# Sums of w_in earlier on VectorE, one first-layer block behind the x transposes of units 2 and 3, and values and masks of units 4 to 7 in another order

## The chip, the core and the metric

One core of one Trainium2 chip runs the whole program. The core has a matrix engine (TensorE; its matmuls are called PE in the profile, its weight loads PEld), VectorE (DVE), ScalarE (ACT), GpSimd (POOL) and SyncE (SP), each with its own instruction queue, and 16 DMA engines that carry the transfers which POOL, SP and ACT issue. The metric is the device time of one execution in microseconds. A change under about 0.3% can't be told from none here.

## What is computed

The inputs q, k and v have the shape (8, 8, 576, 64): batch, heads, positions, head dimension. Attention looks at a window of 32 positions on both sides. Its output, one row of 512 per token, goes through a two-layer network with a GELU in its sigmoid form.

```python
scores = scale * np.matmul(q, k.transpose(0, 1, 3, 2))
mask = np.abs(pos[:, None] - pos[None, :]) <= 32
attn = softmax(np.where(mask, scores, -1e9))
x = np.matmul(attn, v).transpose(0, 2, 1, 3).reshape(4608, 512)
h = x @ w_in                              # 512 x 2048
g = h * (1.0 / (1.0 + np.exp(-1.702 * h)))
out = g @ w_out                           # 2048 x 512
```

## The kernel before

**Units and tiles.** The 4608 tokens are cut into 36 units of 128 and 9 tiles of 512 (four units). For a unit `u` the steps are: `scores(u)` (24 small matmuls, then two exponentials on ACT, one for each half of the heads, which write the tile `p`), `band(u)` (VectorE multiplies `p` by the 0/1 mask), `values(u)` (TensorE multiplies `p` with the values), `norm(u)` (VectorE divides by the row sums and writes `x`), and a transpose of `x` into `xT`. Each unit is worked in blocks of 64 positions, so `values(u)` needs the values twice: `ve[u % 9]`, the 128 rows as loaded, and `vo[u % 5]`, the 128 rows from 64 further on. `odd_v(u)` makes `vo` with two copies: rows 64 to 127 of `ve[u]`, and rows 0 to 63 of `ve[u + 1]`.

**PSUM.** Every accumulator lies in one of seven named places: `t` (two banks) and `A`, `C`, `B`, `E`, `LA`, `LB`. A step that writes one must wait until the last reader of the step before it in that place is done. `scores(u, "t")` and `values(u, "t")` take `t`; with `"AC"` they take A and C, one for each half of the heads.

**The first layer.** Tile 0 goes through `layer1_plain(0, d, half, tag)` (line 378): eight matmuls for 256 of the 2048 hidden columns (block d of 0 to 7) and 256 of the tile's tokens, then a GELU on ACT. In `opening`, `l1(half, *ds)` calls it with the places of the list `h` in turn. From tile 1 on, `l1_group` (line 407) computes with seven products instead of eight. Four of these need sums of w_in, the tiles `a1` to `a4`, and sums of x (`xs`). `w1_sums((i,), half)` (line 327) makes half of one of the four with one VectorE instruction. Half 0 reads the chunks 0 and 2 of w_in (512 columns each), half 1 the chunks 1 and 3. The first use of the sums is in the first group of tile 1.

**The second layer.** For tile 0 `self.l2` is a list of 64 steps of one matmul each, worked off by `self.do(self.l2, n)` between other work. The steps 0 to 7 need chunk 0 of w_out (`w2`), 8 to 15 chunk 1, 16 to 23 chunk 2, 24 to 31 chunk 3.

**What sets the order.** The program is written in a manual schedule: each engine executes its instructions in the order in which the code calls them, and waits in that order. So the position of a call in `opening` (line 562) is its position on every engine that it uses, and an instruction that waits holds back everything behind it on its engine.

**Loads.** q, k, v, w_in and w_out are loaded and converted by DMAs that POOL issues in program order. In the program's list of waits eight completion counters take turns, so every such load waits, before it is issued, for the load that stands eight places before it on POOL. The loads around the change are, in this order: w_in chunk 3, v 5, v 6, w_out chunk 0, v 7, v 8, w_out chunks 1, 2, 3, k 8, q 8 (two pieces), k 9, v 9, q 9, k 10, v 10.

**The stage of the change.** `opening` builds tile 0 (units 0 to 3) and the attention of tile 1 (units 4 to 7). Its second half, from line 644 on, runs: block 4 of half 0, the transposes of x of units 2 and 3 (`x_T2`, line 313, copied to `xT` by VectorE), the two copies `k_first` and `v_first`, then the blocks of half 1 between the transposes of tile 1's k and q (`T_four`, line 181: 32 transposes, two copies each), block 5 of half 0, scores of units 4 and 5, the blocks 6 and 7, the scores of units 6 and 7, eight steps of layer 2, then the masks, values and norms of units 4 to 7, two more blocks, and the transposes of x of units 4 to 7. Then `first_layer1` (line 847) begins tile 1's first layer.

Of the kernel before, what the change touches and what calls it, by code (L numbers as in the profile page):

```python
# [26 lines left out]
class _Kernel:  # L27
# [166 lines left out]
    def load_v(self, u):  # L194
        if u >= self.NU:
            return
        t = self.ve[u % 9]
        for off, b, s, n in self.pieces(128 * u, 128):
            self.nc.gpsimd.dma_start(t[off:off + n, :, :self.D], self.v[b, :, s:s + n, :].rearrange("h s d -> s h d"))  # L199

    def odd_v(self, u, eng):

        vo = self.vo[u % 5]
        nxt = self.v_first if u == self.NU - 1 else self.ve[(u + 1) % 9][0:64]

        def words(ap):
            return ap.rearrange("p h d -> p (h d)").bitcast(I32)

        eng.tensor_copy(words(vo[64:128]), words(self.ve[u % 9][64:128]))  # L209
        eng.tensor_copy(words(vo[0:64]), words(nxt))  # L210
# [351 lines left out]
    def opening(self):  # L562

        nc, dve, act, pool = self.nc, self.nc.vector, self.nc.scalar, self.nc.gpsimd
        self.setup()
        dve.memset(self.idle, 0.0)
        dve.memset(self.spark, 0.0)
        for t in self.ve:
            dve.memset(t[:, :, self.D:], 1.0)
        self.load_first("k", 0)  # L570
        self.load_first("q", 0)
        make_identity(nc, self.ident)
        act.activation(self.spark, self.spark, AF.Exp)
        for u in (0, 1, 2):
            self.load_v(u)
        self.load_w1(0)
        self.setup_mask()
        self.load_first("k", 1)
        self.load_first("q", 1)
        self.cut_mask()  # L580
        self.load_w1(1)
        self.load_v(3)
        self.load_v(4)
        self.load_w1(2)
        self.load_four("k")
        self.load_four("q")
        self.load_w1(3)
        self.odd_v(3, pool)
        dve.tensor_copy(self.identh, self.ident)
        self.keep_busy(60, "E", 96)  # L590
        self.T_first("k", 0, "AC", (dve, act))
        self.keep_busy(6, "E")
        self.T_first("q", 0, ("LA", "LB"), (dve, act))
        self.keep_busy(4, "E")
        for u in (5, 6):
            self.load_v(u)
        self.load_w2(0)
        for u in (7, 8):
            self.load_v(u)
        for c in (1, 2, 3):  # L600
            self.load_w2(c)
        self.load_kq("k", 8)
        self.scores(0, "t")
        self.scores(1, "AC")
        self.odd_v(0, dve)
        self.odd_v(1, dve)
        self.keep_busy(10, "E")
        self.band(0)
        self.band(1)
        self.values(0, "t")  # L610
        self.values(1, "AC")
        self.norm(0)
        self.norm(1)
        self.keep_busy(6, "E")
        self.x_T(0, "LA", act)
        self.keep_busy(4, "E")
        self.x_T(1, "LB", act)
        self.T_first("k", 1, "AC", (dve, dve))
        h, n, gelus = [], [0], []

        def l1(half, *ds):
            for d in ds:
                self.layer1_plain(0, d, half, h[n[0] % len(h)])
                n[0] += 1

        self.layer1_plain(0, 0, 0, "B", gelus)
        self.T_first("q", 1, ("LA", "LB"), (dve, act))
        self.layer1_plain(0, 1, 0, "E", gelus)
        h[:] = ["B", "E", "LB"]
        self.scores(2, "t")  # L630
        self.scores(3, "AC")
        self.layer1_plain(0, 2, 0, "LA", gelus)
        self.layer1_plain(0, 3, 0, "LB", gelus)
        self.do(gelus)
        self.band(2)
        self.odd_v(2, dve)
        self.band(3)
        self.keep_busy(4, "t")
        self.values(2, "t")
        self.norm(2)  # L640
        self.keep_busy(4, "A")
        self.values(3, "AC")
        self.norm(3)
        l1(0, 4)
        self.x_T2(2, "A", dve)
        dve.tensor_copy(self.k_first, self.kT[0][:, :, 0:64])
        dve.tensor_copy(self.v_first, self.ve[0][0:64])
        for u in (8, 9, 10, 11):
            self.fetch(u)
        l1(1, 0, 1)  # L650
        halo = self.kT[4]
        self.T_four("k", "AC", (dve, dve))
        dve.tensor_copy(self.kT[4][:, :, 0:64], halo)
        l1(1, 2, 3)
        l1(0, 5)
        self.T_four("q", "AC", (dve, act))
        l1(1, 4, 5)
        self.odd_v(4, dve)
        self.scores(4, "t")
        self.scores(5, "AC")  # L660
        for i in (3, 1, 2, 4):
            self.w1_sums((i,), 0)
        self.odd_v(5, dve)
        for d, tag in ((6, "B"), (7, "E")):
            self.layer1_plain(0, d, 0, tag, gelus)
        self.do(self.l2, 3)
        self.scores(6, "t")
        self.do(self.l2, 3)
        self.scores(7, "AC")
        self.do(gelus)  # L670
        self.do(self.l2, 2)
        self.band(4)
        self.band(5)
        self.odd_v(6, dve)
        self.odd_v(7, dve)
        self.band(6)
        self.values(4, "t")
        self.norm(4)
        self.band(7)
        self.values(5, "AC")  # L680
        self.norm(5)
        self.do(self.l2, 8)
        self.values(6, "t")
        self.norm(6)
        self.values(7, "AC")
        self.norm(7)
        h[:] = "BE"
        n[0] = 0
        for i in (3, 1):
            self.w1_sums((i,), 1)  # L690
        l1(1, 6, 7)
        self.x_T2(4, "A", act)
        self.do(self.l2, 4)
        self.x_T2(6, "t", dve)
        self.do(self.l2, 4)
# [218 lines left out]
```

## Time and profile before

| what | us |
|---|---|
| median of three runs (lowest, highest) | 287.91 (287.08, 288.02) |
| the profiled execution | 287.27 |
| its span in the trace | 285.5 |
| PE busy in the span | 275.4 |
| DVE busy | 217.1 |
| ACT busy | 193.7 |
| POOL busy | 128.3 |

The granted TensorE clock was 0.997 of full speed. The profile has these views: busy time and the chain of work that ended last; a timeline (start, duration in us, engine, line, operation, output<-inputs, and in brackets the idle time of that engine before it with what ended the wait); busy times of all engines in chosen windows; and the DMA issues. A row that ends in xN merges N like instructions. A row of POOL with DMA_DIRECT2D is the issuing of a load, and not its transfer: the landing shows only in what waits for it.

### The profile page before, as it was taken

The page shows a single profiled execution, that of the slowest core. Times are in us where ns is not written, and L with a number is a line of the kernel's source. Part 1 is how long each engine was busy: PE and PEld are TensorE (multiplying, and loading weights), DVE is VectorE, ACT ScalarE, POOL GpSimd, SP SyncE. Part 2 cuts the span into 40 slices and gives each one's busy share as a digit, 9 for nine tenths or more (in the row PEclk, how much of TensorE's full clock was granted, in tenths as well). Part 3 has the DMA queues.
Part 4 walks back from the last instruction along what each step waited for, and adds up shares of the span by engine and source line. Part 5 has one row for each costly group of instructions (what it writes and reads, how often), then busy time and mean ns, then how long its engine had stood idle before and what let it go on. Part 6 is the DMA issues. An engine that isn't in the chain of part 4 may idle for free.

```text
span 285.5 us, 9217 instructions
## 1 busy us (share of the span) xinstructions
PE 275.4 (96%) x3818; PEld 230.0 (81%) x3818; DVE 217.1 (76%) x500; ACT 193.7 (68%) x340; POOL 128.3 (45%) x194
## 2 busy tenths in 40 slices
PE   7898999999999999999999999999999999999994
PEld 6676847776778888888888888888887888888883
DVE  1755898897887978797879787888778878945731
ACT  2565784789787769667966896588658865568410
POOL 8966546898588538948175819330110000000000
PEclk9999999999999999999999999999999999999998
DMA  8999999999999999999999999994422030101033
GB/s 94 185 193 199 183 205 156 191 123 129 121 147 151 163 149 193 162 186 134 194 133 208 125 195 99 200 110 115 130 57 82 16 110 21 73 2 73 2 112 115
DMA packets 146987, 37.38 MB, mean 131 GB/s; under 512 B 133888, under 2 KB 142592, under 8 KB 146944
## 3 DMA queue, kind: packets, MB, share of 16 engines
q0 software_dynamic: 104464, 18.42, 95.7%
q1 hardware_dynamic: 42032, 17.84, 34.0%
q8 instruction: 30, 0.49, 0.7%
q10 hardware_dynamic: 448, 0.52, 0.6%
q14 instruction: 13, 0.11, 0.1%
HBM read 36.83 MB, written 9.44 MB: 162 GB/s over the span
## 4 chain that ended last, share of the span: by engine, by line
PE 83%; DVE 6%; ACT 4%; POOL 2%; DMA 2%; issue 2%; POOLq 0%
PE h L70 38%; PE o L70 37%; PE pv L70 3%; PE sc L70 3%; DMA kq<-in_k_dram 2%; ACT p L256 2%; DVE x L294 1%; DVE p L264 1%; PE tp L322 1%; POOL ve L199 1%; PE tp L232 1%; DVE a L335 1%; DVE vo L209 1%; ACT g L419 1%; PE tp L189 1%
## 5 line engine op out<-in xcount | busy, mean ns | idle before, releaser
L419 ACT ACTIVATE g<-h 128x512 f16<-128x512 f32 x128 | 72.2, 598 | 36.2 <-PE h L70 35.4
L70 PEld LDWEIGHTS <-g 128*128 128x128 f16 x576 | 54.5, 98 | 9.7
L70 PEld LDWEIGHTS <-a 128*128 128x128 f16 x512 | 49.3, 97 | 11.3 <-issue 1.2
L70 PE MATMUL h<-xs,a 128*128 128x256 f16 x384 | 57.6, 272 | 0.4 <-DVE h L432 0.2
L70 PEld LDWEIGHTS <-w 128*128 128x128 f16 x512 | 48.9, 98 | 7.9 <-DVE xT L67 1.0
L70 PE MATMUL o<-w,g 128*128 128x256 f16 (+1 forms) x320 | 55.1, 294 | 0.0
L70 PE MATMUL h<-xT,w 128*128 128x256 f16 x384 | 54.0, 273 | 1.1 <-DVE xT L67 0.8
L199 POOL DMA_DIRECT2D ve<-in_v_dram x40 | 34.0, 853 | 34.5 <-issue 26.4
L70 PEld LDWEIGHTS <-gs 128*128 128x128 f16 x384 | 36.8, 98 | 5.2 <-issue 0.6
L256 ACT ACTIVATE p<-sc 128x512 bf16<-128x512 f32 x72 | 36.6, 621 | 3.2 <-PE sc L70 3.2
L70 PE MATMUL o<-b,gs 128*128 128x256 f16 x256 | 37.6, 273 | 0.5 <-ACT o L67 0.5
L70 PE MATMUL o<-b,g 128*128 128x256 f16 x256 | 37.3, 273 | 0.0
L432 DVE TENSOR_TENSOR h<-h,s 128x512 f32<-128x512 f32 x32 | 22.3, 698 | 18.6 <-PE h L70 18.4
L131 POOL DMA_DIRECT2D qst<-in_q_dram x35 | 28.1, 805 | 6.1 <-DMA w<-in_moe_w_out_dram 3.0
L131 POOL DMA_DIRECT2D kst<-in_k_dram x31 | 26.4, 855 | 7.9 <-DMA ve<-in_v_dram 3.6
L67 ACT COPY h<-h 128x512 f32<-128x512 f32 x32 | 18.9, 589 | 15.9 <-PE h L70 15.5
L294 DVE TENSOR_TENSOR x<-pv,rec 128x256 f16<-128x256 f32 (+1 forms) x53 | 27.5, 520 | 1.8
L264 DVE TENSOR_TENSOR p<-p,mask 128x1024 bf16<-128x1024 bf16 x36 | 24.6, 685 | 3.1 <-ACT p L256 3.1
L438 DVE TENSOR_TENSOR h<-h,s 128x512 f32<-128x512 f32 x32 | 22.4, 699 | 4.8 <-PE h L70 4.2
L209 POOL COPY vo<-ve 64x264 int32<-64x264 int32 x29 | 13.8, 478 | 26.3 <-PE pv L70 24.8
L67 ACT COPY s<-h 128x512 f32<-128x512 f32 x32 | 19.2, 599 | 1.4
L70 PE MATMUL h<-xs,w 128*128 128x256 f16 x128 | 19.2, 273 | 0.0
(85 smaller groups left out, 366.5 us busy)
## 6 DMA issues: line engine op xcount, KB each, us to landing
out_dram<-o_sb SPq DMA_DIRECT2D x33, 256.0 KB, 3.9
ve<-in_v_dram POOLq DMA_DIRECT2D x32, 128.0 KB, 7.1
kst<-in_k_dram POOLq DMA_DIRECT2D x25, 128.0 KB, 6.8
qst<-in_q_dram POOLq DMA_DIRECT2D x21, 128.0 KB, 6.6
w<-in_moe_w_in_dram POOLq DMA_DIRECT2D x4, 512.0 KB, 8.6
w<-in_moe_w_out_dram POOLq DMA_DIRECT2D x4, 512.0 KB, 12.9
qst<-in_q_dram POOLq DMA_DIRECT2D x7, 96.0 KB, 7.7
kq<-in_q_dram POOLq DMA_DIRECT2D x2, 256.0 KB, 6.0
```

The source lines that it names most:

```text
L67: (eng.copy if eng is self.nc.scalar else eng.tensor_copy)(out, in_)
L70: self.nc.tensor.matmul(out, lhsT, rhs, start=start, stop=stop, skip_group_check=True)
L131: self.nc.gpsimd.dma_start(t[off:off + n], src[b, :, s:s + n, :].rearrange("h s d -> s h d"))
L189: self.nc.tensor.transpose(tp[64 * (h % 2):64 * (h % 2) + 64, h // 2, j, :], src[:, 4 * i + h, j, :], self.ident)
L199: self.nc.gpsimd.dma_start(t[off:off + n, :, :self.D], self.v[b, :, s:s + n, :].rearrange("h s d -> s h d"))
L209: eng.tensor_copy(words(vo[64:128]), words(self.ve[u % 9][64:128]))
L256: self.nc.scalar.activation(p[:, eo].rearrange("k h s -> k (h s)"), sc[eo], AF.Exp, scale=self.scale)
L264: (eng or self.nc.vector).tensor_mul(pv, pv, msk.to_broadcast([128, 8, 2, SQ]))
L294: dve.tensor_mul(x[:, 4 * at:4 * (at + n), :].rearrange("p (b h) d -> p b h d", b=n), acc[:, :, :, :D], r.to_broadcast([128, n, 4, D]))
L419: act.activation(g[:, f, 256 * half:256 * half + 256], bank.rearrange("p (i n) -> p i n", i=2), AF.Gelu_apprx_sigmoid)
L432: dve.tensor_add(e, b, s7)
L438: dve.tensor_add(c, b, s7)
```

## The change

Five things move, in `opening`, and one helper is new; nothing is computed differently.

1. `l1(0, 5)`, block 5 of half 0 of tile 0, moves from behind `l1(1, 2, 3)` to directly behind `x_T2(2, "A", dve)`. The list of places grows from three (B, E, LB) to four (B, E, LB, LA).
2. The half-0 sums of w_in move: 3, 1, 2 to behind the copies `k_first` and `v_first`, 4 to behind the copies of tile 1's k. They stood between `odd_v(4)` and `odd_v(5)`.
3. The half-1 sums 3 and 1 move from behind `norm(7)` to behind `odd_v(5)`, which so moves forward itself.
4. `odd_v(6)` and `odd_v(7)` move ahead of `band(5)`; each later mask moves behind the norm of an earlier unit; the eight layer-2 steps between `values(5)` and `values(6)` become four there and four behind `norm(6)`.
5. The load of v 8 is cut into two of 64 rows, and chunk 1 of w_out is issued between the two.

```diff
+    def load_v_part(self, lo, n):
+        u, at = divmod(lo, 128)
+        t = self.ve[u % 9]
+        for off, b, s, m in self.pieces(lo, n):
+            self.nc.gpsimd.dma_start(t[at + off:at + off + m, :, :self.D],
+                                     self.v[b, :, s:s + m, :].rearrange("h s d -> s h d"))
...
         self.load_w2(0)
-        for u in (7, 8):
-            self.load_v(u)
-        for c in (1, 2, 3):
+        self.load_v(7)
+        self.load_v_part(1024, 64)
+        self.load_w2(1)
+        self.load_v_part(1088, 64)
+        for c in (2, 3):
             self.load_w2(c)
...
-        h[:] = ["B", "E", "LB"]
+        h[:] = ["B", "E", "LB", "LA", "B", "E", "LB", "LA"]
...
         l1(0, 4)
         self.x_T2(2, "A", dve)
+        l1(0, 5)
         dve.tensor_copy(self.k_first, self.kT[0][:, :, 0:64])
         dve.tensor_copy(self.v_first, self.ve[0][0:64])
+        for i in (3, 1, 2):
+            self.w1_sums((i,), 0)
...
         dve.tensor_copy(self.kT[4][:, :, 0:64], halo)
+        self.w1_sums((4,), 0)
         l1(1, 2, 3)
-        l1(0, 5)
         self.T_four("q", "AC", (dve, act))
         l1(1, 4, 5)
         self.odd_v(4, dve)
         self.scores(4, "t")
         self.scores(5, "AC")
-        for i in (3, 1, 2, 4):
-            self.w1_sums((i,), 0)
         self.odd_v(5, dve)
+        for i in (3, 1):
+            self.w1_sums((i,), 1)
...
         self.band(4)
-        self.band(5)
         self.odd_v(6, dve)
         self.odd_v(7, dve)
-        self.band(6)
+        self.band(5)
         self.values(4, "t")
         self.norm(4)
-        self.band(7)
+        self.band(6)
         self.values(5, "AC")
         self.norm(5)
-        self.do(self.l2, 8)
+        self.band(7)
+        self.do(self.l2, 4)
         self.values(6, "t")
         self.norm(6)
+        self.do(self.l2, 4)
         self.values(7, "AC")
         self.norm(7)
         h[:] = "BE"
         n[0] = 0
-        for i in (3, 1):
-            self.w1_sums((i,), 1)
         l1(1, 6, 7)
```

## The prediction, made before the result was known

> **What bounds the kernel now.** I read the page first (span, and the chain that ended last), then busy times in windows, to see in which stage TensorE is not full.
>
> ```profile
> span 285.5 us, 9217 instructions
> ...
> PE 83%; DVE 6%; ACT 4%; POOL 2%; DMA 2%; issue 2%; POOLq 0%
> ```
> ```profile
> 22.00:45.00 23.00, 21.21 (x360) 15.87 (x360) 18.16 (x41) 15.73 (x26) 11.26 (x15) 1.00 1.56 192
> 45.00:69.20 24.20, 24.18 (x206) 17.58 (x203) 20.61 (x39) 18.74 (x34) 22.34 (x30) 1.00 2.01 150
> ...
> 90.00:285.50 195.50, 191.31 (x2425) 165.50 (x2423) 150.87 (x350) 131.21 (x234) 61.97 (x94) 1.00 1.12 117
> ```
>
> The columns are the window, its length, then busy time of PE, PEld, DVE, ACT, POOL, clock, DMA. From 45 us on TensorE is the bound (24.18 of 24.20 us, then 191.31 of 195.50). Between 22 and 45 us, the stage of the change, it is idle for 1.79 us, and some of its busy time there is spread-out small matmuls that wait. Whatever reaches the end of this stage earlier passes on to the end, as long as the loads allow it. So the question is how much earlier the blocks 6 and 7 of half 1 start, which close the attention of units 4 to 7. The chain that ended last tells where that stands:
>
> ```profile
> 31.33 0.48 DVE kq L67
> ...
> 43.00 0.32 PE pv L70 x8
> 43.32 1.85 PE h L70 x16
> ...
> 45.62 0.86 PE o L70 x4
> ```
>
> Those two blocks are the 16 matmuls at 43.3; the chain comes to them over VectorE, from 31.33 on. Four layer-2 steps take 0.86 us. The first place where time is lost is seen on TensorE:
>
> ```profile
> 22.73 1.05 PE L70 MATMUL h<-xT,w 128*128 128x256 f16 x8 [0.27 <-ACT g L390]
> 23.61 0.61 PE L322 MATMUL tp<-identh,x 128*128 128x128 f16 x8
> 25.01 1.92 PE L70 MATMUL h<-xT,w 128*128 128x256 f16 x16 [0.79 <-DVE xT L67]
> 26.86 1.11 PE L189 MATMUL tp<-ident,o_sb 128*64 128x128 bf16 x32
> 27.90 2.79 PE L70 MATMUL h<-xT,w 128*128 128x256 f16 x24
> 30.62 1.11 PE L189 MATMUL tp<-ident,o_sb 128*64 128x128 bf16 x32
> 31.67 1.92 PE L70 MATMUL h<-xT,w 128*128 128x256 f16 x16
> 33.52 0.70 PE L70 MATMUL sc<-kq 64*64 64x64 bf16 x48
> ```
>
> After the x transposes (23.61) TensorE stands idle 0.79 us for VectorE's copy of xT. Block 5 is the third part of the 24 matmuls at 27.90.
>
> **Part 1: block 5 into the gap.** Eight such matmuls take 22.73 to 23.61, 0.88 us. In the new order they begin when the transposes end (25.01 less 0.79, 24.2) and end near 25.0, where the copy of xT lets the next block start anyway. Its weights are there (block 4, same chunk, runs at 22.73). The 24 matmuls become 16, so everything from 30.62 on may come 0.88 us earlier: q transposes at 29.74, scores of units 4 and 5 at 32.64. The longer list of places costs nothing: all four have been read by GELUs of earlier blocks, and layer 2, which takes LA and LB, comes after them.
>
> **Part 2: does VectorE keep up until the scores?**
>
> ```profile
> 25.00 0.28 DVE L647 COPY v_first<-ve 64x528 bf16<-64x528 bf16 x1
> 27.56 2.35 DVE L67 COPY kq<-tp 128x1024 bf16<-128x1024 bf16 x2 [2.28 <-PE tp L189]
> 29.84 0.21 DVE L653 COPY kq<-kq 128x256 bf16<-128x256 bf16 x1
> 31.33 1.22 DVE L67 COPY kq<-tp 128x1024 bf16<-128x1024 bf16 x1 [1.28 <-PE tp L189]
> 32.59 0.69 DVE L209 COPY vo<-ve 64x264 int32<-64x264 int32 x1
> 33.31 0.29 DVE L210 COPY vo<-ve 64x264 int32<-64x264 int32 x1
> 33.52 1.28 DVE L335 TENSOR_TENSOR a<-w 128x1024 f16<-128x1024 f16 x2
> ...
> 35.56 0.69 DVE L336 TENSOR_TENSOR a<-w,a 128x1024 f16<-128x1024 f16 x1
> 36.27 0.72 DVE L209 COPY vo<-ve 64x264 int32<-64x264 int32 x1
> ```
>
> Three sums take 33.52 to 35.56, 2.04 us. Behind v_first they fill 25.3 to 27.3 of an idle stretch that ends at 27.56: nothing is late; if they were slowed by half, the k copies would be 0.8 us late, and the cover behind them (below) would be used up. The fourth sum runs 30.05 to 30.75. The q copy, ready at 31.33 less 0.88, 30.45, so starts 0.3 us late and ends at 31.97; the scores want it at 32.64, so 0.6 us of cover is left. Then come `odd_v(4)`, `odd_v(5)` and two sums of half 1 (1.28): 0.98 + 1.0 + 1.28 = 3.3 us, until 35.3. The first mask can't start before that anyway:
>
> ```profile
> 35.53 4.03 ACT L256 ACTIVATE p<-sc 128x512 bf16<-128x512 f32 x8
> ```
>
> Eight exponentials, 0.504 us each, stand behind a table load and the GELUs of the blocks before; all of these come 0.88 us earlier, so they start at 34.65 and finish units 4, 5, 6, 7 at 35.66, 36.67, 37.67, 38.68. Units 6 and 7 reuse t, A and C, and `values(4)` waits for t, too: this chain on ACT gains 0.88 us and no more, however early VectorE is.
>
> **Part 3: masks, values, norms.**
>
> ```profile
> 38.55 0.30 DVE L209 COPY vo<-ve 64x264 int32<-64x264 int32 x1
> ...
> 39.73 0.68 DVE L264 TENSOR_TENSOR p<-p,mask 128x1024 bf16<-128x1024 bf16 x1
> 40.34 0.19 DVE L293 RECIPROCAL rec<-pv 128x8 f32<-128x8 f32 x1
> 40.56 0.69 DVE L294 TENSOR_TENSOR x<-pv,rec 128x512 f16<-128x512 f32 x1
> 41.17 0.68 DVE L264 TENSOR_TENSOR p<-p,mask 128x1024 bf16<-128x1024 bf16 x1
> 41.77 0.17 DVE L293 RECIPROCAL rec<-pv 128x4 f32<-128x4 f32 x1
> ...
> 42.86 0.20 DVE L293 RECIPROCAL rec<-pv 128x8 f32<-128x8 f32 x1
> ```
>
> From start to start: a mask 0.61 (39.73 to 40.34), a norm from t 0.83 (40.34 to 41.17), a norm from A and C 1.09 (41.77 to 42.86), four copies of `odd_v` 1.18 (38.55 to 39.73). In the new order: band 4 35.7 to 36.3; four copies to 37.5; band 5 to 38.1. `values(4)` starts when t is free (37.67, and about 0.15 on) and takes 0.6, so norm 4 starts at 38.45. From there VectorE has no gap: 0.83 + 0.61 (band 6) + 1.09 (norm 5) + 0.61 (band 7) = 3.14, to 41.6. `values(7)` needs that mask, takes 0.45 with the latency, and blocks 6 and 7 start at 42.15 in place of 43.25 (the row of the chain says 43.32, after the last values): **1.1 us earlier**. The half-1 sums are gone from behind norm 7; the two blocks on TensorE (1.85 us) covered their 1.28 us there, so that gives nothing more.
>
> **Part 4: loads and contention.**
>
> ```profile
> 19.93 0.41 POOL L209 COPY vo<-ve 64x264 int32<-64x264 int32 x1 [0.44 <-DMA ve<-in_v_dram]
> 20.40 0.40 POOL L210 COPY vo<-ve 64x264 int32<-64x264 int32 x1
> ...
> 35.15 0.58 POOL L131 DMA_DIRECT2D qst<-in_q_dram  x1 [1.18 <-DMA w<-in_moe_w_out_dram]
> 36.01 0.89 POOL L131 DMA_DIRECT2D kst<-in_k_dram  x1 [0.28 <-DMA ve<-in_v_dram]
> 37.10 0.88 POOL L199 DMA_DIRECT2D ve<-in_v_dram  x1 [0.21 <-DVE vo L209]
> 39.81 0.87 POOL L131 DMA_DIRECT2D qst<-in_q_dram  x1 [1.83 <-DMA w<-in_moe_w_out_dram]
> ```
>
> Since each issue waits for the load eight places before, these rows give landings: w_out chunk 0 at 35.1, v 7 at 36.0, v 8 by 37.1, chunk 1 at 39.8. `odd_v(6)` and `odd_v(7)` now want v 7 at 36.6 and the first half of v 8 at 37.2: both are there. The first layer-2 steps come at 35.0, with chunk 0 landing at 35.1, in front of scores that wait until 35.66 anyway: hidden. Steps 8 to 11 come at 39.0 and want chunk 1. It is passed by half a v load. A half load's price: v 3 ended POOL's wait at 19.93, and the first half of v 4 was there by 20.40, so at most 0.47 us; a whole one is about 0.9 (v 7). Chunk 1 so lands near 39.35, and steps 8 to 11 run to 40.25. `values(6)` follows, four more steps end at 41.5, still before band 7 (41.6): no cost. [...] POOL issues one load more (0.6 to 0.9 us), in time in which it waits; k 8 to k 9 are first used in the second group of the stage that begins at 45 us, and v 8's second half only for unit 8.
>
> VectorE's copies are another matter: 0.30 us with POOL at rest (38.55), but 0.72 beside POOL's issue of 36.01, and 0.69 at 32.59. In the new order POOL issues the two loads of 36 to 37.5 just beside the four copies that are now ahead of band 5. Bounds: no copy hit, 0; two hit, 2 x 0.42 = 0.84. Norm 4 waits for `values(4)` for 0.3 us after band 5, so 0 to 0.5 us of it reaches the path. I take 0.1 (one copy hit).
>
> **Sum.** 1.1 less 0.1: a gain of 1.0 us. On the profiled execution that is 287.27 - 1.0 = 286.3; its span would be 284.5. The median of the three runs lies 0.64 above it, the mean of all four executions is 287.57, and I set the gain against that mean: **286.6 us**.
>
> **Rivals.**
>
> *A: the contention takes more.* Two copies hit, 0.5 us on the path, and the fourth sum or the q copy a little late (cover 0.6): a gain of 0.5 to 0.8, 286.8 to 287.1. For: four copies beside two issues. Against: the copy at 33.31 ran in 0.29 although POOL was issuing.
>
> *B: slower, the values load becomes the wait.* `odd_v(7)` now stands ahead of band 5, and every later mask and norm stands behind it on VectorE. From 37.5 on each us by which the first half of v 8 lands late moves the whole chain by one. Break-even is a landing at 38.6; if the half load is only done with chunk 1 behind it (39.8), the chain is 2.3 us late less the gain of 1.1: 288.8. For: a load completes only with its last piece. Against: 37.1 for the whole of v 8 now.
>
> *C: a half load costs a whole.* Chunk 1 at 39.8: steps 8 to 11 end at 40.7, `values(6)` at 41.15, the other four steps at 42.05, then `values(7)`: 0.35 to 0.45 us of the gain goes, which leaves 0.6 to 0.7, 286.9. Against: the row of 20.40.
>
> *D: VectorE was the whole bound, as the chain paints it.* Then 2.6 us of sums off it give 2 us, 285.5. Against: the exponentials beside it.
>
> **How the numbers follow.** Forecast 0.55 (gain 0.85 to 1.2), A 0.22, C 0.08, B 0.09, D 0.06. 0.3% is 0.86 us: faster by more is the forecast and D, 0.61; within, A and C, 0.30; slower, B, 0.09. The range reaches down to 285.8 (a gain of 1.1 on the fastest run is 286.0, and a little of D) and up to 287.6 (A's 0.5 on the median is 287.4); B and most of D are left out.
>
> **What would show it.** In the new profile: no idle time of 0.79 on TensorE before the block at 25.0; the k copies still near 27.6; scores of unit 4 near 32.6; exponentials from 34.7; band 5 done by 38.6, and blocks 6 and 7 at 42.1 to 42.3. Copies of `vo` at 0.7 before band 5 speak for A; VectorE idle behind a DMA in `odd_v(7)` for B; TensorE idle at 39 to 39.9 on w_out for C. A gain at 45 us that is gone at 70 us would mean that the later loads, and not TensorE, set the pace.

## The result, and the profile after

The changed kernel takes 286.25 us in the median of seven runs (285.84 to 286.63); the kernel before 287.40 (286.83 to 288.02), also in the median of seven, three of which are those of the table above. The ratio is 0.9953 with a 95% interval of 0.9937 to 0.9969: 1.15 us less, beyond the 0.3% that can be told from no change. The profiled execution took 286.05 us with a span of 284.3, against 287.27 and 285.5.

TensorE's timeline of the changed kernel, in the stage that the prediction works on (start, duration, engine, line, operation):

```profile
22.84 1.05 PE L70 MATMUL h<-xT,w 128*128 128x256 f16 x8
23.73 0.61 PE L329 MATMUL tp<-identh,x 128*128 128x128 f16 x8
24.18 2.87 PE L70 MATMUL h<-xT,w 128*128 128x256 f16 x24
...
32.76 0.70 PE L70 MATMUL sc<-kq 64*64 64x64 bf16 x48
...
39.40 1.04 PE L70 MATMUL o<-w,g 128*128 128x512 f16 x4
...
42.53 0.72 PE L70 MATMUL h<-xT,w 128*128 128x256 f16 x5
```

The wait of 0.79 us is gone: 24 matmuls follow the transposes at 24.18. Since the whole stage starts 0.11 us later than in before, I measure from the first of these rows (block 4 of half 0) to the last (blocks 6 and 7 of half 1): 42.53 - 22.84 = **19.69 us**, in before 43.25 - 22.73 = **20.52**. So the stage gives 0.83 us in this pair of profiled runs. VectorE's timeline of the changed kernel tells where it could have been more:

```profile
25.32 1.28 DVE L342 TENSOR_TENSOR a<-w 128x1024 f16<-128x1024 f16 x2
26.64 0.69 DVE L342 TENSOR_TENSOR a<-a,w 128x1024 f16<-128x1024 f16 x1
27.68 2.36 DVE L67 COPY kq<-tp 128x1024 bf16<-128x1024 bf16 x2 [0.35 <-PE tp L189]
...
33.26 1.28 DVE L342 TENSOR_TENSOR a<-w 128x1024 f16<-128x1024 f16 x2
35.97 0.69 DVE L271 TENSOR_TENSOR p<-p,mask 128x1024 bf16<-128x1024 bf16 x1 [1.43 <-ACT p L263]
36.69 0.46 DVE L216 COPY vo<-ve 64x264 int32<-64x264 int32 x1
37.18 0.29 DVE L217 COPY vo<-ve 64x264 int32<-64x264 int32 x1
37.50 0.55 DVE L216 COPY vo<-ve 64x264 int32<-64x264 int32 x1
38.07 0.29 DVE L217 COPY vo<-ve 64x264 int32<-64x264 int32 x1
38.29 0.68 DVE L271 TENSOR_TENSOR p<-p,mask 128x1024 bf16<-128x1024 bf16 x1
38.89 0.19 DVE L300 RECIPROCAL rec<-pv 128x8 f32<-128x8 f32 x1
```

VectorE waits 1.43 us for the exponentials ahead of band 4 and has no gap from there to norm 4 (nor behind it, to the last mask); the four copies between band 4 and band 5 take 1.60 us (36.69 to 38.29). The chain that ended last runs through exactly these rows.

Of the 1.19 us by which the span is shorter, 0.72 are there where the next stage scores unit 8 (first two fences: before, then after) and 0.83 at 188 us; the rest comes between 188 and 216 us, which the prediction doesn't speak of:

```profile
69.24 0.70 PE L70 MATMUL sc<-qT,kT 64*64 64x64 bf16 x48
...
188.33 0.70 PE L70 MATMUL sc<-qT,kT 64*64 64x64 bf16 x48
...
214.49 0.60 PE L70 MATMUL h<-xs,a 128*128 128x256 f16 x4 [0.23 <-DVE h L432]
...
216.41 0.70 PE L70 MATMUL sc<-qT,kT 64*64 64x64 bf16 x48
```
```profile
68.52 0.67 PE L70 MATMUL sc<-qT,kT 64*64 64x64 bf16 x46
...
187.50 0.70 PE L70 MATMUL sc<-qT,kT 64*64 64x64 bf16 x48
...
213.30 0.60 PE L70 MATMUL h<-xs,a 128*128 128x256 f16 x4
...
215.22 0.70 PE L70 MATMUL sc<-qT,kT 64*64 64x64 bf16 x48
```

From the scores at 188 to those at 216 us before takes 28.08 us, after 27.72. No call of that part of the program is changed. TensorE waits in before for an addition of VectorE (`h<-h,s`, line 432). That addition follows ACT's copy of the product that it adds. ACT's and VectorE's rows for it, before and after:

```profile
212.67 0.58 ACT L67 COPY s<-h 128x512 f32<-128x512 f32 x1
```
```profile
213.74 0.70 DVE L432 TENSOR_TENSOR h<-h,s 128x512 f32<-128x512 f32 x1 [1.09 <-PE h L70]
```
```profile
211.83 0.59 ACT L67 COPY s<-h 128x512 f32<-128x512 f32 x1
```
```profile
212.55 0.70 DVE L439 TENSOR_TENSOR h<-h,s 128x512 f32<-128x512 f32 x1 [0.74 <-PE h L70]
```

In before the addition starts 1.07 us after that copy, in after 0.72: it is 0.35 us late in before, and nothing that it reads explains it.

### The profile page after: what moved, and what is told of

The parts are those of the page before. It is cut to its first block, busy times and chain, and to the rows that moved or that the text cites. A ratio compares the mean times of both kernels' runs of the same rounds, so it can differ in the third digit from the quotient of the medians.

```text
span 284.3 us, 9219 instructions
## 1 busy us (share of the span) xinstructions
PE 275.4 (97%) x3818; PEld 229.8 (81%) x3818; DVE 217.0 (76%) x500; ACT 193.7 (68%) x340; POOL 128.8 (45%) x195
## 4 chain that ended last, share of the span: by engine, by line
PE 87%; DVE 4%; ACT 3%; DMA 2%; issue 1%; POOL 1%; DVEq 0%; ACTq 0%; POOLq 0%
PE h L70 39%; PE o L70 37%; PE pv L70 4%; PE sc L70 3%; DMA ve<-in_v_dram 2%; DVE p L271 2%; DVE x L301 1%; ACT p L263 1%; PE tp L329 1%; ACT L263 1%; PE junk L70 1%; PE tp L189 1%; PE tp L239 1%; POOL ve L199 1%; ACT g L426 1%
## 5 line engine op out<-in xcount | busy, mean ns | idle before, releaser
L199 POOL DMA_DIRECT2D ve<-in_v_dram x39 | 33.3, 857 | 37.8 <-issue 30.8
```

## The experiments

Two theories stood behind them. The first is the prediction's, cut to size: block 5 in the gap is the stage's gain, and the copies ahead of band 5 lie on the path. The second came from the rows above: the 0.36 us that before loses late have to do with the two halves of v 8, the one part of the change that adds instructions. Rivals are named with each run. Executions of one kernel differ by 1 us and more (before beside c1_after: 286.89 to 289.04); in some profiled runs part of this is seen as TensorE's wait for late transposes by DMA after 100 us (0.37 us in c0_before, 0.43 in e3_oldmasks, 0.76 in e9_oddpool_one). So beside each time stand two lengths from the trace that this doesn't touch: the stage, and the stretch from 188 to 216 us. "Gap" is the time from VectorE's wait to the start of the addition near 214 us, by the trace's records of VectorE. The experiments were taken in three groups, each with runs of before beside it, and the group e4 to e7 on another chip than the other two: a time is to be compared within its group, or through the ratio. (The ratio on record is not exactly the quotient of the two medians.)

| run | stage, us | 188 to 216, us | gap, ns | median, us (runs) | before beside it | ratio (95%) |
|---|---|---|---|---|---|---|
| before, profiled | 20.52 | 28.08 | 415 | 287.40 (7) | | |
| after, profiled | 19.69 | 27.72 | 64 | 286.25 (7) | 287.40 | 0.9953 (0.9937 to 0.9969) |
| c0_before | 20.35 | 28.07 | 416 | 287.8 (1) | 287.39 | |
| e1_block | 19.76 | 28.07 | 416 | 286.88 (12) | 287.39 | 0.9985 (0.997 to 1.000) |
| e2_sums | 20.35 | 28.08 | 417 | 287.31 (12) | 287.39 | 0.9998 (0.9981 to 1.0016) |
| e3_oldmasks | 19.48 | 27.71 | 65 | 286.42 (7) | 287.39 | 0.9959 (0.9941 to 0.9977) |
| e4_wholev8 | 19.54 | 28.07 | 417 | 286.83 (10) | 288.00 | 0.9955 (0.9933 to 0.9977) |
| e5_vo6early | 19.24 | 27.72 | 65 | 286.65 (12) | 288.00 | 0.9954 (0.9928 to 0.9981) |
| e6_oddpool | 18.72 | 27.72 | 65 | 285.74 (7) | 288.00 | 0.9914 (0.9886 to 0.9943) |
| e7_block_split | 19.73 | 27.71 | 65 | 285.97 (6) | 288.00 | 0.9921 (0.9895 to 0.9947) |
| e8_one_more | 20.35 | 27.72 | 64 | 287.11 (12) | 287.44 | 0.9991 (0.9972 to 1.0009) |
| e9_oddpool_one | 18.73 | 27.72 | 65 | 285.53 (11) | 287.44 | 0.9943 (0.9925 to 0.9960) |
| c1_after | 19.75 | 27.72 | 65 | 286.10 (6) | 287.44 | 0.9952 (0.9935 to 0.9969) |

One thing enters the stages beside the edits. The loads don't move with the stage: POOL's wait for chunk 0 of w_out ended at 35.67 us in after, whose stage starts at 22.84, and at 35.63 in e4_wholev8, whose stage starts at 23.30. In three of the profiled runs TensorE waited for chunk 0 ahead of the first layer-2 steps: 0.40 us in after, 0.53 in e7_block_split and 0.62 in c1_after. The row in after:

```profile
35.43 0.33 PEld L70 LDWEIGHTS <-g 128*128 128x128 f16 x3 [0.40 <-DMA w<-in_moe_w_out_dram]
```

Counted from the start of the stage, `values(4)` is then done at 15.83, 15.96 and 16.05 us, and at 15.54 to 15.57 in the six other runs that have block 5 in the gap. Norm 4 can't come before these values. In e1_block, e3_oldmasks and e7_block_split it comes much later (16.56 us or more), and the chunk changes nothing. But in e4_wholev8, e5_vo6early, e6_oddpool and e9_oddpool_one it comes at 15.58 to 15.90, in after at 16.05 and in c1_after at 16.09; so a part of what these four gain in the stage over the changed kernel may belong to the chunk and not to the edit.

### c0_before: the kernel before, once more

> The kernel before once more, for its trace. In the first trace the gain was 0.72 us at 69 us and 0.83 at 188 us, and another 0.36 us came between 195 us and the end, where TensorE waited 0.23 us for VectorE's sum at 214.5. If that is a property of the kernel before, the wait stands there again and the span is near 285.5; if it is scatter between executions, the wait is elsewhere or missing and the span is up to 0.4 us shorter or longer. The measure should be 20.4 to 20.6 us.

Measured: 287.8 us, the stage 20.35 us (a little under the 20.4 expected at least), and the addition late again; the span of 286.1 us is longer than expected. The profiled run of before had two of its copies of `vo` at 0.69 and 0.72 us beside POOL's issues; here the slowest takes 0.58. So the stage of before takes 20.35 us when it is little disturbed (e2_sums and e8_one_more give the same), and 0.17 of the 0.83 us belong to that one run: the disturbed run of before on which the prediction, too, built its sum.

### e1_block: block 5 alone

```diff
-        h[:] = ["B", "E", "LB"]
+        h[:] = ["B", "E", "LB", "LA", "B", "E", "LB", "LA"]
...
         self.x_T2(2, "A", dve)
+        l1(0, 5)
...
         l1(1, 2, 3)
-        l1(0, 5)
```

> The kernel before, with part 1 alone: block 5 of half 0 stands directly behind the x transposes of units 2 and 3, and the list of places has four entries; sums, masks and loads stay as before. The measure is the time in the trace from the start of block 4 of half 0 (8 matmuls) to the start of blocks 6 and 7 of half 1 (16 matmuls): 20.52 us in the kernel before, 19.69 in the changed one. Theory (the block in the gap moves TensorE and with it the exponentials; VectorE has room enough even with the sums between): the scores of unit 4 come 0.88 us earlier, VectorE reaches mask 4 at about its exponential, and the measure is 19.6 to 19.9, so part 1 alone gives 0.65 to 0.95 us of time, nearly the whole of the change. Rival (VectorE is the bound, and the sums have to leave its chain first): the measure stays within 0.3 us of 20.52 and the time within 0.3 us.

Measured: the stage takes 19.76 us, as expected, which is all that the whole change reaches in c1_after (19.75). The time fell by 0.51 us, less than the 0.65 to 0.95 expected. The expectation counted from the 20.52 us of the disturbed run; from 20.35 the stage gives 0.59. The addition near 214 us is still late, as in before.

### e2_sums: the sums alone

```diff
         dve.tensor_copy(self.v_first, self.ve[0][0:64])
+        for i in (3, 1, 2):
+            self.w1_sums((i,), 0)
...
         dve.tensor_copy(self.kT[4][:, :, 0:64], halo)
+        self.w1_sums((4,), 0)
...
-        for i in (3, 1, 2, 4):
-            self.w1_sums((i,), 0)
         self.odd_v(5, dve)
+        for i in (3, 1):
+            self.w1_sums((i,), 1)
...
-        for i in (3, 1):
-            self.w1_sums((i,), 1)
         l1(1, 6, 7)
```

> The kernel before, with the moves of the sums alone (half 0 behind v_first and behind the copies of k, half 1 with odd_v(5) ahead of the masks); block 5 stays behind l1(1, 2, 3), masks and loads as before. Theory (the exponentials on ACT hold the masks, and they don't move): mask 4 at 36.7 in place of 37.2, mask 5 still waits for its exponential, and the measure (block 4 to blocks 6 and 7, 20.52 us before) is 20.15 to 20.35, so the time falls by 0.2 to 0.35 us only. Rival (the chain that ended last ran over VectorE through 2.6 us of sums, and these were the bound): the measure falls by 1.2 us or more.

Measured: 20.35 us, the same as c0_before's, and the same time, where a fall of 0.2 to 0.35 us was expected. VectorE's rows show where the freed time went, into a wait for the exponentials ahead of bands 4 and 5:

```profile
36.93 0.69 DVE L264 TENSOR_TENSOR p<-p,mask 128x1024 bf16<-128x1024 bf16 x1 [1.21 <-ACT p L256]
37.84 0.69 DVE L264 TENSOR_TENSOR p<-p,mask 128x1024 bf16<-128x1024 bf16 x1 [0.22 <-ACT p L256]
```

So VectorE alone was not the bound; the chain of before, which ran over VectorE, had ACT's exponentials right beside it.

### e3_oldmasks: the change without its new order of masks and values

```diff
         self.band(4)
+        self.band(5)
         self.odd_v(6, dve)
         self.odd_v(7, dve)
-        self.band(5)
+        self.band(6)
         self.values(4, "t")
         self.norm(4)
-        self.band(6)
+        self.band(7)
...
-        self.band(7)
-        self.do(self.l2, 4)
+        self.do(self.l2, 8)
         self.values(6, "t")
         self.norm(6)
-        self.do(self.l2, 4)
```

> The changed kernel with part 4 undone: masks, odd_v(6), odd_v(7), values, norms and the eight layer-2 steps stand in the old order. Theory (VectorE does the same work from mask 4 to norm 7 in either order, so only waits inside it count): the four copies come behind mask 5, where POOL still issues loads; the measure is 19.6 to 19.9, against 19.69, and the time is within 0.2 us of the changed kernel. Rival (the new order is what lets norms 4 and 5 come early, and without it the gain goes): the measure is 20.2 or more and the time 0.5 us or more above the changed kernel.

Measured: 19.48 us, a little under the range expected, so the new order isn't needed, and between these two runs it was 0.2 us the worse one: here, behind bands 4 and 5 the four copies come after POOL's issues and take 0.29 us each. The times (0.9959 beside 0.9953) are alike.

### e4_wholev8: the change with v 8 in one load

```diff
-        self.load_v_part(1024, 64)
-        self.load_w2(1)
-        self.load_v_part(1088, 64)
-        for c in (2, 3):
+        self.load_v(8)
+        for c in (1, 2, 3):
             self.load_w2(c)
```

> The changed kernel with v 8 loaded whole again, and chunks 1, 2 and 3 of w_out behind it. Theory: the stage is shortened by the block in the gap and hardly by the split, so from block 4 of half 0 to blocks 6, 7 of half 1 it still takes 19.6 to 19.9 us (before 20.35 to 20.52, after 19.69), chunk 1 landing some 0.5 us later beside the wait for the probabilities; what the split does lies late: the 0.23 us wait of TensorE near 214 us, and the 0.36 us more between the scores at 188 and those at 216 us, are back, so the time is 0.3 to 0.4 us above the changed kernel's. Rival (the split is needed by w_out): the stage is longer by 0.35 us or more with TensorE waiting for w_out near 39.5 us, and nothing comes back at 214 us.

Measured: the stage takes 19.54 us, no more than with the halves, and the late addition is back. TensorE's row near 214 us:

```profile
214.06 0.60 PE L70 MATMUL h<-xs,a 128*128 128x256 f16 x4 [0.23 <-DVE h L439]
```

The time doesn't show it by itself: beside before the ratio (0.9955) is that of the changed kernel (0.9953), which was taken in another group. Within its own group the median is 0.86 us over e7_block_split's; 0.36 of that is seen in this stretch, and the profiled run's stage also started 0.64 us later than e7_block_split's (23.30 and 22.66).

### e7_block_split: before, with the block and the two halves of v 8 only

The edit is that of e1_block, with the loads cut as in the change.

> Before, with the block in the gap (and the list of the four places that are left) and the two halves of v 8, without the other orders of sums, masks and values. Theory: the stage is that of the block alone (19.6 to 19.9 us), and the split takes the 0.36 us late: no wait of TensorE near 214 us, time within 0.3 us of the changed kernel's. Rival (the split does nothing late): time like the block alone, 0.5 to 0.7 us above the changed kernel's, with the wait near 214 us.

Measured: stage 19.73, stretch 27.71, no wait; the interval of the ratio (0.9895 to 0.9947) lies wholly under e1_block's, though the difference is larger than 0.36 us, and what the rest is stays open. Here, too, the late 0.36 us are gone with the halves of v 8; what in the halves does it, this run can't tell.

### e5_vo6early: a copy in front of band 4

The first copy of `odd_v(6)` needs only v 6, so it can run where VectorE waits for the exponentials.

```diff
+    def odd_v(self, u, eng, part=(0, 1)):
...
+        self.odd_v(6, dve, (0,))
         for d, tag in ((6, "B"), (7, "E")):
...
         self.band(4)
-        self.odd_v(6, dve)
+        self.odd_v(6, dve, (1,))
         self.odd_v(7, dve)
```

> The changed kernel with the first copy of odd_v(6), which needs v 6 alone, in front of band 4, where VectorE waits 1.43 us for the exponentials. Theory (the copies between bands 4 and 5 stand on the path with their whole length): the stage is 0.2 to 0.45 us shorter (19.25 to 19.5 us), and the time by as much. Rival (norm 4 waits for the values anyway, the 0.3 us of slack that the prediction counted): the stage is within 0.1 us of the changed kernel's 19.69.

Measured: 19.24 us, 0.45 under 19.69. VectorE's rows from the wait to norm 4:

```profile
36.26 0.29 DVE L217 COPY vo<-ve 64x264 int32<-64x264 int32 x1
38.16 0.69 DVE L273 TENSOR_TENSOR p<-p,mask 128x1024 bf16<-128x1024 bf16 x1 [1.60 <-ACT p L265]
38.77 0.28 DVE L219 COPY vo<-ve 64x264 int32<-64x264 int32 x1
39.08 0.29 DVE L217 COPY vo<-ve 64x264 int32<-64x264 int32 x1
39.41 0.29 DVE L219 COPY vo<-ve 64x264 int32<-64x264 int32 x1
39.62 0.68 DVE L273 TENSOR_TENSOR p<-p,mask 128x1024 bf16<-128x1024 bf16 x1
40.24 0.21 DVE L302 RECIPROCAL rec<-pv 128x8 f32<-128x8 f32 x1
```

Three copies now stand between the two masks, none of them slowed, and norm 4 still follows band 5 without a wait. That the copies are on the path with their whole length doesn't follow from the 0.45, because two other things differ. TensorE didn't wait for chunk 0 here, so `values(4)` was done 15.54 us after the stage's start, and norm 4 came at 15.58. In after the values were done at 15.83 and norm 4 came at 16.05, so there an earlier band 5 could have brought norm 4 forward by about 0.2 us. And band 4 itself started late: it is record 63 of VectorE in this run, and by the trace's records it starts 462 ns after its wait, in after 66. The 1.60 us in its row hold these 0.40 us. They cost nothing here, as norm 4 would else have waited for the values.

The median (286.65) doesn't show it; this kernel's stage started at 24.66 us in the profiled run, and its runs lie between 285.82 and 288.42.

### e6_oddpool: the copies for units 6 and 7 on POOL

```diff
-        for u in (8, 9, 10, 11):
+        self.load_kq("q", 8)
+        self.odd_v(6, pool)
+        self.odd_v(7, pool)
+        self.load_kq("k", 9)
+        self.load_v(9)
+        for u in (9, 10, 11):
             self.fetch(u)
...
         self.band(4)
-        self.odd_v(6, dve)
-        self.odd_v(7, dve)
         self.band(5)
+        self.band(6)
         self.values(4, "t")
```

The rest of the order of masks and values is that of e3_oldmasks.

> The changed kernel with the order of masks and values of before, and with all four copies for units 6 and 7 on POOL, between its issues of q 8 and k 9. Theory: without the copies VectorE's bands and norms follow the exponentials directly, the last band is done 0.6 us or more earlier, and the stage takes 18.9 to 19.3 us, the time some 0.4 to 0.7 us below the changed kernel's, if POOL's later issues keep ahead. Rival: the copies on POOL are slow enough for values(6) and (7), or the loads of units 8 and 9 behind them come late, and the stage or the marks behind it (scores of unit 8) are no earlier than the changed kernel's.

Measured: 18.72 us, more than expected. VectorE's masks each wait for their exponentials, and ACT sets the pace:

```profile
36.87 0.69 DVE L271 TENSOR_TENSOR p<-p,mask 128x1024 bf16<-128x1024 bf16 x1 [1.17 <-ACT p L263]
37.78 0.69 DVE L271 TENSOR_TENSOR p<-p,mask 128x1024 bf16<-128x1024 bf16 x1 [0.22 <-ACT p L263]
38.76 0.69 DVE L271 TENSOR_TENSOR p<-p,mask 128x1024 bf16<-128x1024 bf16 x1 [0.29 <-ACT p L263]
39.37 0.20 DVE L300 RECIPROCAL rec<-pv 128x8 f32<-128x8 f32 x1
```

And a new row near 159 us: one group earlier, the same addition is now 0.35 us late there.

```profile
159.24 0.60 PE L70 MATMUL h<-xs,a 128*128 128x256 f16 x4 [0.23 <-DVE h L439]
```

That turned the second theory into one that can be counted. Counted from 0 with its waits, VectorE has 589 records in before and 590 with the halves of v 8: one wait more. The late addition is record **447** in before, c0_before, e1_block, e2_sums and e4_wholev8, and 448, and on time, in every run with 590. In e6_oddpool (587 records) the late one, with 418 ns from its wait, is record **319** = 447 - 128. The addition near 214 us is record 445 there and on time, but record 446 behind it, a wait that starts 72 to 77 ns after the addition in all other runs so far, starts 427 ns after it: the 0.35 us are still there, in the shadow of the addition, which takes 0.7 us.

### e8_one_more and e9_oddpool_one: one tiny copy more on VectorE

```diff
+        one = self.sb("one", [128, 4], BF16, 1)
+        dve.tensor_copy(one, self.k_first[:, 0, 0:4])
         self.band(4)
```

In e8_one_more this edit is made to before, in e9_oddpool_one to e6_oddpool.

> Before, with one tiny copy (128 x 4) more on VectorE, ahead of band 4, where VectorE waits for the exponentials anyway: nothing of the change is in it. Theory (a seam in VectorE's own program: its instruction number 447, counted from 0 with its waits, starts 0.35 us late in every run without the second half load of v 8, and there it is the add behind ACT's s7 copy near 214 us; one instruction more ahead of it lets the seam fall on the wait in front of that add, where it is hidden): from block 4 of half 0 to blocks 6, 7 of half 1 it takes 20.35 to 20.5 us as before, the 0.23 us wait of TensorE near 214 us is gone, from the scores at 188 to those at 216 us it takes 27.72 instead of 28.08 us, and the time is 0.3 to 0.4 us under before. Rival (the second half load itself, by POOL or the DMA queue, takes the 0.36 us): the wait stays, 28.07 us, and the time is that of before.

Measured, with nothing of the change in the kernel: the stage stays at 20.35 us, and the addition near 214 us is on time. ACT's copy and VectorE's addition:

```profile
212.74 0.59 ACT L67 COPY s<-h 128x512 f32<-128x512 f32 x1
```
```profile
213.47 0.70 DVE L432 TENSOR_TENSOR h<-h,s 128x512 f32<-128x512 f32 x1 [0.74 <-PE h L70]
```

The start is 0.73 us behind the copy, and 188 to 216 us takes 27.72 us. The median is 0.33 us under before, as expected, though the interval of the ratio (0.9972 to 1.0009) would not show that by itself. The rival, that the second load takes the 0.36 us, is out: this kernel has no second load.

> The kernel with the four copies for units 6 and 7 on POOL, with the same tiny copy on VectorE. In that kernel, which has three instructions fewer on VectorE, the 0.35 us falls on number 319 instead, the add near 158 us. Theory: one instruction more takes the wait there away and brings it to no other place; the stage stays at 18.7 us, and the time is 0.3 to 0.4 us under that kernel's (285.3 to 285.5 us). Rival: the wait at 159 us stays, or another comes, and the time is that kernel's 285.74.

Measured: the stage 18.73 us, no late addition at either place. The addition near 214 us is record 446 here, and it is the wait behind it, record **447**, that starts 430 ns after it. But the theory that the wait comes at no other place is wrong: the tiny copy made band 4 record **63** = 447 - 3 x 128, and band 4 starts 479 ns after its wait, in e6_oddpool 65. The stage takes this up, since bands 5 and 6, which waited 0.22 and 0.29 us for their exponentials in e6_oddpool, now follow without a wait. The time of 285.53 us is at the edge of what was expected. The profiled run lost 1.0 us elsewhere, between 132 and 160 us, where k's transpose by DMA came late:

```profile
135.89 0.44 PE L70 MATMUL sc<-qT,kT 64*64 64x64 bf16 x22 [0.76 <-DMA kT<-kst]
```

The runs lie between 285.01 and 287.14, four of eleven under 285.2. The median is the lowest of all kernels here: 1.9 us under before and 0.57 under the changed kernel on the same chip. The intervals of the two ratios overlap, so that it beats the changed kernel is shown for the stage (1.0 us, a part of which may be chunk 0's), and only likely for the time.

### c1_after: the changed kernel beside them

> The changed kernel again, beside the other two on one chip. Theory: the stage takes 19.7 us, no wait near 214 us, and the time is 0.4 to 0.5% under before. By the terms so far (0.8 us in the stage, 0.36 us late) that is some 0.8 us under the kernel with one tiny copy more, and some 0.8 to 1.0 us above the one with the copies on POOL and the tiny copy.

Measured: stage 19.75, time 1.34 us under before: 0.60 from the stage (20.35 to 19.75), 0.36 late, and a rest of 0.4 that no single row carries. It lies 1.0 us under e8_one_more, where 0.8 was expected, and 0.57 above e9_oddpool_one, where 0.8 to 1.0 was.

## Why the prediction was right, and where it was not

**The time** was put at 286.6 us and came out at 286.25; the forecast gain of 1.0 us was 1.15. But this is two terms, one smaller than forecast and one that the prediction doesn't have: 0.6 to 0.83 us from the stage, and 0.36 us from a late VectorE instruction near 214 us. That their sum came so near 1.0 is luck.

**Part 1, block 5 in the gap: right.** Scores of unit 4 at 32.76, less the later start of 0.11: 32.65, forecast 32.64. e1_block shows that it carries the stage's gain nearly alone: 19.76 beside 19.75 in c1_after, and beside 19.48 and 19.54 in e3_oldmasks and e4_wholev8, which have the sums moved too and didn't wait for chunk 0. So in these runs the other parts add 0.2 to 0.3 us at most.

**Part 2, VectorE keeps up: right.** The sums fill 25.32 to 27.3, the k copies start at 27.68, the exponentials at 34.78 (34.67 on before's time, forecast 34.65).

**Part 3 and the contention of part 4: right that copies would run long, wrong on what that costs.** Band 5 was to start at 37.5 and started at 38.29, on before's time 38.18: 0.68 late. Of this 0.16 come ahead of band 4 (35.86 for 35.7: the way from ACT's last write to VectorE was left out), 0.11 between band 4 and the first copy (0.72 from start to start, counted as 0.61), and 0.42 from copies that ran long beside POOL's issues (35.67 to 37.95): 1.60 us for four copies in place of 1.18. That 0.42 is the very size that was put on one hit copy, though spread over two (0.46 and 0.55). The term that failed is the slack of 0.3 us ahead of norm 4. 0.27 us of small terms had used most of it up before the contention came, so that norm 4 was 0.33 us late, and not 0.1. And the slack moved: e5_vo6early and e6_oddpool run norm 4 some 15.6 us after the stage's start, as the forecast had it (38.45 - 22.73 = 15.72), but in the changed kernel `values(4)` itself was done only at 15.83, and in c1_after at 16.05, where norm 4 (16.09) waited 0.08 us for it. So in after the copies set norm 4, and in c1_after the values. Blocks 6 and 7 started 0.27 us later than forecast (42.42 on before's time, for 42.15, which leaves out the 0.1 for contention). One slip stands in the sum: 41.6 and 0.45 make 42.05, and not 42.15; the difference is about what a mask takes (0.68) beyond its 0.61 from start to start.

**Part 4, the loads: right for chunk 1, wrong for chunk 0.** Steps 8 to 11 of layer 2, which want chunk 1 of w_out, run at 39.40 straight behind the values of unit 5, in c1_after at 39.20; forecast was a landing near 39.35, and 39.8 if a half load cost a whole. By the profile's DMA issues chunk 1 landed 13.0 us after its issue at 26.55 in before, and 12.2 us after its issue at 26.87 in after: some 0.4 us earlier, as forecast. In rival C, where a half costs a whole, chunk 1 would land at 39.8 and still have been out at 39.20; here the measurement decides against it. The step that failed is chunk 0: the prediction called its landing hidden, and TensorE waited 0.40 us for it in after and 0.62 in c1_after, which is what moved `values(4)`. What the two halves cost together can be read on POOL, where k 10 waits for chunk 2:

```profile
42.11 0.88 POOL L131 DMA_DIRECT2D kst<-in_k_dram  x1 [1.43 <-DMA w<-in_moe_w_out_dram]
```
```profile
42.37 0.88 POOL L131 DMA_DIRECT2D kst<-in_k_dram  x1 [0.94 <-DMA w<-in_moe_w_out_dram]
```

Before, then after: 0.26 us later. But POOL's issue behind chunk 0, which is ahead of both halves, came 0.52 us later in after (35.67 for 35.15), so these rows show no cost of the cut. That the cut was needed is another question: e4_wholev8 does without it and its stage is not longer.

**What the prediction missed.** "POOL issues one load more (0.6 to 0.9 us), in time in which it waits" counted the second half for POOL and for the loads behind it. But with it one wait more comes into VectorE's program (near 70 us, by the records of e7_block_split beside those of e1_block), and this instruction was left out. And "From 45 us on TensorE is the bound" was read from busy shares of long windows; the wait of 0.23 us at 214.49 stood in the timeline of before and was not seen in a share of 191.31 in 195.50.

**The rivals.** A (contention takes more) is half true: two copies were hit, but by 0.17 and 0.26 us and not by 0.42 each, and 0.33 us of it reached norm 4. B didn't come: the first half of v 8 landed 10.4 us after its issue at 26.19, near 36.6, and the copy at 38.07, which wants it, ran with no wait. B's argument, that a load completes only with its last piece, is seen on chunk 1 in before: by the trace's records its 16 pieces landed from 35.88 to 39.52, and POOL's wait for it ended at 39.81. C didn't come. D is refuted by e2_sums: the half-0 sums gone from ahead of the masks, with the shorter half-1 sums in their place, gave nothing by themselves, and VectorE waited for the exponentials.

## What to carry to other kernels

An instruction that needs nothing from the wait in front of it belongs into that wait: with all four copies off VectorE's path (e6_oddpool) the stage was the shortest (18.72 us), while the new order of masks, values and norms with all its parts showed no gain. Before a gain of a few tenths in a stage is put down to an edit, see whether the loads landed as early in both runs, counted from the stage's start. Slack of a few tenths is to be spent first on the small gaps between instructions, and only then on a risk such as contention. And when a program gets or loses instructions on an engine, compare a late stretch that the edit doesn't touch: a gain or loss there of always the same size (here 0.36 us) may come from where the instructions fall in the engine's program, and one tiny instruction more tells, as in e8_one_more. It can also move the late one onto another path, as it did in e9_oddpool_one with band 4, which started 479 ns after its wait.

## What the runs showed of the hardware

**A seam in VectorE's program.** At certain places in VectorE's program, counted in its instructions and not in its work, an instruction starts 0.35 to 0.41 us late: record 447 in before, c0_before, e1_block, e2_sums, e4_wholev8 and e9_oddpool_one, 319 and 446 in e6_oddpool (127 apart; a record may be missing between them), and 63, which is band 4, in e5_vo6early and e9_oddpool_one. 63, 319 and 447 lie whole multiples of 128 apart. It is seen only where the late one stands right behind a wait (or is itself the wait behind such an addition); in before record 319 stands in the middle of a norm and starts 34 ns after the one ahead of it is done. It lay on the path only as an addition: in the five profiled runs where that fell near 214 us, the stretch took 28.07 or 28.08 us, in the eight others 27.71 or 27.72. Where record 447 is the wait ahead of the addition, nothing is seen (in after the addition starts 64 ns behind the wait's start), since the engine waits there anyway; where it is the wait behind it, the addition hides it. What happens at the seam is not shown. The queue that the profile calls "q14 instruction" (0.11 MB in 13 packets) moved a packet of 8 KB at 214.95 us in before, half a microsecond behind the end of the late addition, and one at 208.23 in after, where nothing is late near 214 us. In before, from 214.5 to 215:

```profile
q14 instruction: 1, 0.01, 4.0%
```

No run here tells whether the packet has to do with the late start.

**Copies beside POOL's issues.** A copy of `vo` took 0.29 to 0.30 us on VectorE with POOL at rest (before, 38.55 to 39.52); beside an issue some took as little (before, 33.31: 0.29), and others up to 0.72 (before, 36.27). On POOL itself, in e6_oddpool, they took 0.40 to 0.92:

```profile
38.79 0.92 POOL L216 COPY vo<-ve 64x264 int32<-64x264 int32 x1
39.78 0.40 POOL L217 COPY vo<-ve 64x264 int32<-64x264 int32 x1
```

There they were slow, and the stage was still the shortest: no other engine waited for them.
